# Nine blocks of dense weights converted during attention instead of ten, with other spacing of the conversions and of the early expert tiles

## The chip, the cores and the metric

The kernel runs on one core of one Trainium2 chip. The metric is the device time of one execution in microseconds (us). The kernel before takes 627.92 us, the median of three runs (627.23 to 629.49).

A core has five engines that work side by side, each through its own instructions in a fixed order: PE (TensorE, matmuls), DVE (VectorE), ACT (ScalarE), POOL (GpSimd) and SP (SyncE, which here only issues transfers). An instruction that waits holds up everything behind it on its engine. Transfers run on 16 DMA engines that all queues share. SBUF is the memory on the chip, PSUM the one that PE writes its results to.

## The reference

Three stages follow each other. Inputs are float32; the dense weights of the third stage arrive as 64-bit numbers.

```python
# 1 attention: 4 batches, 12 heads, 448 positions, 64 wide
scores = cap * np.tanh(scale * q @ k.T / cap)
attn = softmax(scores);  x = attn @ v            # -> 1792 tokens x 768
# 2 soft mixture of 8 experts with 4 slots each
logits = x @ phi                                 # 1792 x 32
d = softmax over tokens;  slot_in = d.T @ x      # 32 x 768
slot_out[e] = relu(slot_in[e] @ w1[e]) @ w2[e]   # w1: 768 x 1024, w2: 1024 x 768
x = softmax over slots(logits) @ slot_out
# 3 dense layers, width 2048
r = relu(x @ w_in);  out = (s * r * r + b) @ w_out
```

## The kernel before

**Stage 1, attention** (0 to 267 us of the profile). The 24 pairs of heads go through PE (scores, L498 and L515), ACT (tanh and exp, L521 and L535), PE again (times v, L556 and L564), and sums on DVE or POOL (L543, L549). Copies out of PSUM (`copy`, L421 on ACT, L423 on DVE) can go to either engine. Each pair loads its q, k and v rows (L432, L437/L438, L441/L446) through SP; there are two buffers for v, so a v load waits until PE has used up the pair two before it.

Two other things are slipped in beside attention. First, **conversions**: the weights of stage 3 are cut into 16 blocks of 128 columns, each block a tile of w_in and one of w_out. A tile arrives as 64-bit words (768 KB, L208). DVE picks the upper words apart in two instructions (L221, L224), ACT turns the lower words into numbers (L231), DVE or POOL adds the two (L234), and the float32 result (384 KB) is stored in a scratch tensor `scr` in DRAM (L342). `XS` is the number of blocks treated so, 2 x XS tiles; the others are converted in stage 3. Second, **early expert tiles**: ten tiles of w1 (1024 KB, L364) and four of w2 (768 KB, L370) are loaded into buffers that exist from the start. Six more w2 tiles have buffers in the space that the conversions use; they can be loaded only after the last conversion is stored (the step `cend`). Still more expert tiles go into space that attention gives up at its end.

**Stage 2, experts** (267 to 342 us). PE reads each expert tile once (L1008 for w1, L1029 for w2); when a tile is used up, its buffer takes the next one.

**Stage 3, dense** (from 342 us). Four passes over up to 512 tokens; in the first pass the 16 blocks must be ready one after the other. A block from `scr` is loaded as float32 (L1117). A block that is not in `scr` is loaded as words (L208) and goes through L221, L224, L231 and L234 here. Then the w_out tile is split into two parts (L1146/L1148, and L1151 on POOL), the w_in tile is multiplied with the slot outputs (L1160 to L1184, result `mst`), and each step x does a matmul (`h`, L1191), five elementwise operations (L1208 to L1236) and 24 large matmuls (`y`, L1254 and L1255).

**What sets the order.** `ListSchedule.run` (top of the file) is a planner that runs on the host while the kernel is built. Each operation has the engines it may run on with a duration in the planner's own units (a third number is a penalty for that engine), a priority, the buffers that it takes (`acq`) and gives back (`rel`), an earliest time (`after`) and a time that its result takes to be there (`lat`). The planner puts every operation behind the last one on its engine, earliest first; what it emits is fixed. It plans stage 1 and stage 3 separately.

The steps that the change touches stand at L293 to L297 (constants), L904 (`pn`), L906 to L912 (conversions: load `cl`, `ca`, `cf`, `cmul`, store `cst`) and L921 to L929 (early expert tiles `W`).

Of the kernel before, what the change touches and what calls it, by code (L numbers as in the profile page):

```python
# [28 lines left out]
ACT, DVE, POOL, PE, SP = "ACT", "DVE", "POOL", "PE", "SP"  # L29
# [73 lines left out]
def kernel(  # L103
# [17 lines left out]
    B, H, S, D = q.shape  # L121
# [45 lines left out]
    wide = w_in.dtype != F32  # L167
# [21 lines left out]
    MC = FF // FC  # L189
    NI = 2 * MC  # L190
    NE1 = KDM * FC
    XS = 10 if wide else 0
    scr_p = ctx.enter_context(tc.tile_pool(name="scr", bufs=1, space=bass.MemoryType.DRAM))
    scr = [scr_p.tile([128, NE1], F32, name=f"scr{i}") for i in range(2 * XS)]

# [97 lines left out]
    def run(safe):  # L293
        W1N, W2N = (4, (4,)) if safe else (10, (4, 6))
        NV, NEB, NES, NXU, NXQ, NQK = 2, 5, 2, 4, 3, 2
        PX, PA, DES, DESL, HACT = -0.32, 2.0, 1.0, 0.5, 0.5
        CV0, CVP, CVA, CVT, WA = 9.33, 2.0, 20.19, 9.5, 30.39  # L297
        LATE = 0.6

        PT, PDEN, PLG, PLW, PXT, PXM, PSO, PSL = -2.67, 1.0, 2.0, 3.4, 3.33, 2.05, 0.25, 4.75  # L300
# [22 lines left out]
        cx = ExitStack()  # L323
        cvs = range(0 if safe else 2 * XS)
        if cvs:
# [24 lines left out]
        def load_next():  # L350
            x = can_load()
            wq.remove(x)
            kind, e, c = x
            i = cnt[kind]
            cnt[kind] += 1
            n = sum(x for _, x in pools[kind])
            i %= n
            for pool, m in pools[kind]:
                if i < m:
                    break  # L360
                i -= m
            if kind == "w1":
                t = pool.tile([128, 2, FE], F32, tag="w1", name="w1c")
                nc.sync.dma_start(  # L364
                    out=t, in_=w1[e, 256 * c:256 * c + 256, :].rearrange("(p k) f -> p k f", p=128)
                )
                w1t[e, c] = t
            else:
                t = pool() if callable(pool) else pool.tile([128, 2, DM], F32, tag="w2", name="w2c")
                nc.sync.dma_start(  # L370
                    out=t, in_=w2[e, 256 * c:256 * c + 256, :].rearrange("(p k) f -> p k f", p=128)
                )
                w2t[e, c] = t
# [381 lines left out]
        def op(name, engs, f, need=(), prio=0.0, acq=(), rel=(), **kw):  # L755
            kw = {"lat": LATE if name[0] not in ("qk", "tanh", "exp", "qkl") else 0.2, **kw}
            sch.add(name, engs, lambda e: f(*name[1:], e), need, prio, acq, rel, **kw)
# [8 lines left out]
        for n in range(NP):  # L766
            f = 2 * n
            for w in "qk":
                i = ("ld", w, n)
# [3 lines left out]
            i = ("ld", "v", n)  # L773
# [58 lines left out]
        for g in range(NQ):  # L832
            bb, gq = divmod(g, NQUAD)
# [58 lines left out]
        for bb in range(B):  # L892
            g = NQUAD * (bb + 1) - 1
            pr = 4 * g + 4 + PSO
            prev = [("ssum", bb - 1)] if bb else []
            op(("soft", bb), [(PE, 0.38)], emit_soft, [("lgr", g)], pr, [("tp", ("soft", bb))], [("lw", g)])
            op(("smax", bb), [(DVE, 0.66)], emit_smax, [("soft", bb)] + prev, pr, [("nm", bb)])
            op(
                ("sexp", bb), [(ACT, 0.8)], emit_sexp, [("smax", bb)], pr, [("pt", bb), ("al", bb)],
                [("tp", ("soft", bb))],  # L900
            )
            op(("ssum", bb), [(DVE, 0.2)], emit_ssum, [("sexp", bb)] + [("pn", bb)] * (bb == B - 1), pr + 1, [], [("nm", bb), ("al", bb)])
            op(("softt", bb), [(PE, 0.33)], emit_softt, [("sexp", bb)], pr, [("tp", ("softt", bb))], [("pt", bb)])
            op(("pn", bb), [(DVE, 0.2)], emit_pn, [("softt", bb)], pr, [("pn", bb)], [("tp", ("softt", bb))])  # L904

        need = []  # L906
        for i in range(len(cvs)):
            pr = CV0 + CVP * i
            op(("cl", i), [(SP, 2.19)], cv_load, [], pr - 6, [("w", i)], lat=3.0, after=CVA + CVT * i)
            op(("ca", i), [(DVE, 1.55)], cv_a, [("cl", i)], pr, [("cm", i), ("ce", i)], [("w", i)], port=BOTH)  # L910
            op(("cf", i), [(ACT, 0.92)], cv_f, [("ca", i)], pr, [], [("w", i)])
            op(("cmul", i), [(DVE, 0.95), (POOL, 1.63)], cv_m, [("cf", i)], pr, [], [("ce", i)], port=BOTH)  # L912
            op(("cst", i), [(SP, 1.1)], cv_store, [("cmul", i)], pr, [], [("cm", i)], lat=LAT)
            need = [("cst", j) for j in range(i + 1)]
# [7 lines left out]
        first, n = W1N + W2N[0], W1N + sum(W2N)  # L922
        prev = []
        for i in range(n):
            sch.add(
                ("W", i), [(SP, 2.91 if i < W1N else 2.19)], lambda e: load_next(),
                prev + [("cend",)] * (i >= first), 1e3 + i, after=WA,
            )
            prev = [("W", i)]  # L929
        sch.run()  # L930
# [177 lines left out]
        def is_words(i):  # L1108
            return wide and (safe or i >= 2 * XS)

# [181 lines left out]
        for i in range(NI):  # L1292
            f, rows = divmod(i, 2)
            pr = float(f)
# [28 lines left out]
        if wide and not safe:  # L1323
            for i in range(NI):
                pr = MC + 2 + i
# [7 lines left out]
        prev = ["sot"]  # L1333
        for x, (t0, n, f) in enumerate(steps):
# [6 lines left out]
            for p in range(parts(x)):  # L1341
                i = (x, p)
# [9 lines left out]
            for t in range(nt):  # L1352
# [7 lines left out]
                prev = [("y", x, t)]  # L1360
# [5 lines left out]
        p2.close()  # L1366

    run(False)
    if dbg is None or "nosafe" not in dbg:
        big = nc.values_load(flag[0:1, 0:1], min_val=0, max_val=1)  # L1370
        with tc.If(big == 1):
            run(True)
# [30 lines left out]
```

## Time and profile before

| | us |
|---|---|
| median of 3 runs | 627.92 |
| the profiled execution | 627.3 |
| its span, first to last instruction | 625.5 |
| PE busy | 574.5 (92%) |
| ACT busy | 388.9 (62%) |
| DVE busy | 374.5 (60%) |
| POOL busy | 141.9 (23%) |
| mean granted TensorE clock | 0.964 |

The span is the time from the first to the last instruction; the execution's own time has 1.8 us around it. The shares of busy time are means over three stages with different limits. The DMA engines moved 139.25 MB, at 223 GB/s on the mean.

### The profile page before, as it was taken

The numbers are of one execution on the slowest core, as the hardware profiler recorded it, in microseconds if no ns is written. First come the engines' busy times: TensorE is split into PE (matmuls) and PEld (weight loads), VectorE is DVE, ScalarE is ACT, GpSimd is POOL, SyncE is SP. The second block draws the span as 40 slices with busy tenths as digits, with TensorE's granted clock in tenths as the row PEclk, the third lists the DMA queues.
The fourth block names the chain that finished last, engine by engine and source line by source line (L and its number), as shares of the span: only waits on it lengthen the run. The fifth ranks groups of instructions, "written<-read, shape, count | busy, mean of one in ns | idle before, by whom it ended". The sixth has DMA issues, their size and how long they took to land.

```text
span 625.5 us, 10133 instructions
## 1 busy us (share of the span) xinstructions
PE 574.5 (92%) x3982; PEld 356.5 (57%) x3982; DVE 374.5 (60%) x543; ACT 388.9 (62%) x550; POOL 141.9 (23%) x84
## 2 busy tenths in 40 slices
PE   6999897999999999799656899999999999999895
PEld 3333232334333433356323688888888888888784
DVE  2586566969999778635400599952676688511211
ACT  3977676778876987200000788886756566665783
POOL 0163264343854425100000824220000000000000
PEclk9999998999999999879977799999999999999998
DMA  8579999995576534999999985500988779000201
GB/s 152 137 236 296 323 287 326 306 269 154 163 240 175 166 97 146 409 418 415 416 418 410 361 298 178 183 2 28 352 276 257 246 254 353 2 2 1 101 1 56
DMA packets 103175, 139.25 MB, mean 223 GB/s; under 512 B 52432, under 2 KB 84944, under 8 KB 100048
## 3 DMA queue, kind: packets, MB, share of 16 engines
q1 hardware_dynamic: 102176, 138.43, 66.5%
q8 instruction: 33, 0.54, 0.3%
q10 hardware_dynamic: 944, 0.10, 0.1%
q14 instruction: 22, 0.18, 0.1%
HBM read 125.14 MB, written 13.37 MB: 221 GB/s over the span
## 4 chain that ended last, share of the span: by engine, by line
PE 61%; DMA 22%; DVE 10%; ACT 3%; issue 2%; SPq 1%; ACTq 0%; DVEq 0%
PE y L1254 25%; PE y L1255 12%; DMA w2c<-in_moe_w_dram 9%; PE sp L498 6%; PE av L556 5%; DMA w<-in_moe_w_in_dram 3%; PE tr L455 3%; DMA w<-scr 2%; DMA vn<-in_v_dram 2%; DMA w<-in_moe_w_out_dram 2%; DVE cm L224 2%; PE gp L1191 2%; DMA woe<-in_moe_w_dram 2%; DVE es L549 1%; PE av L564 1%
## 5 line engine op out<-in xcount | busy, mean ns | idle before, releaser
L1254 PE MATMUL y<-wo,gh 128*128 128x512 f32 x336 | 127.0, 400 | 0.0
L521 ACT ACTIVATE e<-sp,tsc 128x896 f32<-128x896 f32 x84 | 83.3, 1006 | 40.7 <-PE sp L498 28.0
L1236 DVE TENSOR_TENSOR gl<-r,gh 128x512 fp32r<-128x512 f32 (+1 forms) x65 | 42.6, 657 | 99.6 <-ACT r L1221 99.5
L1255 PE MATMUL y<-wo,gh 128*128 128x256 f32 x336 | 94.4, 281 | 0.0
L535 ACT ACTIVATE e<-e,capt 128x896 f32<-128x896 f32 x84 | 84.9, 1040 | 0.4
L498 PE MATMUL sp<-qs,ks 64*128 64x448 f32 x288 | 75.8, 606 | 0.0
L1254 PEld LDWEIGHTS y<-wo,gh 128*128 128x128 f32 x336 | 63.2, 188 | 13.8 <-issue 1.6
L1208 ACT ACTIVATE r<-gp 128x512 f32<-128x512 f32 (+1 forms) x65 | 34.9, 539 | 58.1 <-PE gp L1191 56.4
L556 PE MATMUL av<-e,vn 128*64 128x448 f32 x288 | 69.1, 562 | 1.8 <-DMA vn<-in_v_dram 1.8
L1254 PE MATMUL y<-wo,gl 128*128 128x512 f32 x168 | 66.6, 397 | 0.0
L1255 PEld LDWEIGHTS y<-wo,gh 128*128 128x128 f32 x336 | 63.2, 188 | 1.7
L275 DVE TENSOR_REDUCE rng<-w 128x1 f32<-128x768 f32 x64 | 56.9, 945 | 0.9 <-DMA w<-in_moe_w_in_dram 0.9
L543 POOL TENSOR_TENSOR es<-e 128x896 f32<-128x896 f32 x17 | 38.0, 2233 | 57.3 <-ACT e L535 28.1
L1221 ACT ACTIVATE r<-r,bt,st 128x512 f32<-128x512 f32 (+1 forms) x65 | 49.1, 757 | 1.8
L1221 ACT ACTIVATE gh<-r,bt,st 128x512 fp32r<-128x512 f32 (+1 forms) x65 | 49.1, 757 | 1.6
L1254 PE MATMUL y<-woe,gh 128*128 128x512 f32 x112 | 44.2, 416 | 3.2 <-ACT ob L1272 2.0
L1255 PE MATMUL y<-wo,gl 128*128 128x256 f32 x168 | 47.1, 281 | 0.0
L224 DVE SCALAR_TENSOR_TENSOR cm<-w,cm 128x768 int32<-128x768 int32 x32 | 45.8, 1430 | 1.1
L1146 ACT CAST woe<-w 128x768 fp32r<-128x768 f32 x2 | 1.7, 830 | 71.2 <-DMA w<-scr 71.2
L498 PEld LDWEIGHTS sp<-qs,ks 64*128 64x128 f32 x288 | 23.4, 193 | 35.6 <-issue 12.3
L543 POOL TENSOR_TENSOR es<-es,e 128x896 f32<-128x896 f32 x14 | 32.7, 2337 | 37.7 <-DVE es L543 20.8
L549 POOL TENSOR_TENSOR es<-es,e 64x448 f32<-64x448 f32 x23 | 30.8, 1340 | 42.3 <-DVE es L543 21.7
(153 smaller groups left out, 947.4 us busy)
## 6 DMA issues: line engine op xcount, KB each, us to landing
w<-in_moe_w_in_dram SPq DMA_DIRECT2D x32, 768.0 KB, 5.9
w<-in_moe_w_out_dram SPq DMA_DIRECT2D x32, 768.0 KB, 6.0
w1c<-in_moe_w_dram SPq DMA_DIRECT2D x24, 1024.0 KB, 13.1
w2c<-in_moe_w_dram SPq DMA_DIRECT2D x26, 768.0 KB, 16.5
scr<-cm SPq DMA_DIRECT2D x20, 384.0 KB, 4.4
w<-scr SPq DMA_DIRECT2D x20, 384.0 KB, 5.7
qn<-in_q_dram SPq DMA_DIRECT2D x24, 224.0 KB, 4.2
kn<-in_k_dram SPq DMA_DIRECT2D x24, 192.0 KB, 4.5
```

The source lines that it names most:

```text
L224: nc.vector.scalar_tensor_tensor(out=m, in0=hi, scalar=-0x40000000, in1=m, op0=ALU.bitwise_and, op1=ALU.bitwise_or)
L275: nc.vector.tensor_reduce(out=rng[:, j, i:i + 1], in_=hi, axis=AX.X, op=o, apply_absolute_value=True)
L498: nc.tensor.matmul(out=sp[:, h, 0:S], lhsT=ks[n][rows, 128 * j:128 * j + 128], rhs=qs[n][rows, :], start=True, stop=True,)
L521: nc.scalar.activation(out=e, in_=spt.pop((n, j))[:, :, 0:S], func=AF.Tanh, scale=tsc)
L535: nc.scalar.activation(out=e, in_=e, func=AF.Exp, scale=capt)
L543: eng.tensor_tensor(out=t, in0=et[n, 0] if j == 1 else t, in1=et[n, j], op=ALU.add)
L549: eng.tensor_tensor(out=t, in0=t, in1=et["l", n // 2][r:r + KL, n % 2], op=ALU.add)
L556: nc.tensor.matmul(out=avt[n][64 * h:64 * h + 64, 0:S], lhsT=vt[n][:, KC * h + j, :], rhs=et[n, j][:, h], start=(j == 0 and n % 2 == 0), s ...
L1221: nc.scalar.activation(out=out, in_=in_, func=AF.Identity, scale=st, bias=bt)
L1236: eng.tensor_tensor(out=gl, in0=t, in1=f32(gh), op=ALU.subtract)
L1254: nc.tensor.matmul(out=ya, lhsT=lhsT, rhs=w[:, 0:512], start=first, stop=last)
L1255: nc.tensor.matmul(out=yb, lhsT=lhsT, rhs=w[:, 512:768], start=first and i0 == 0, stop=last and i0 == per - 1)
```

## The change

XS goes from 10 to 9: 18 tiles instead of 20 are converted in stage 1, and block 9 (two tiles) joins the six blocks that are converted in stage 3. The conversions get priorities 1.85 apart instead of 2.0 and earliest times 8.5 apart instead of 9.5. A conversion's load is planned to take 6.0 units to land instead of 3.0. Each early expert tile gets an earliest time of its own, 5.0 units after that of the tile before it. The penalty for a copy on ACT goes from 0.5 to 0.2. The small copy `pn` is planned with 1.2 instead of 0.6 units, but for the last batch.

```diff
-    XS = 10 if wide else 0
+    XS = 9 if wide else 0
...
-        PX, PA, DES, DESL, HACT = -0.32, 2.0, 1.0, 0.5, 0.5
-        CV0, CVP, CVA, CVT, WA = 9.33, 2.0, 20.19, 9.5, 30.39
+        PX, PA, DES, DESL, HACT = -0.32, 2.0, 1.0, 0.5, 0.2
+        CV0, CVP, CVA, CVT, WA, WT = 9.33, 1.85, 20.19, 8.5, 30.39, 5.0
...
-            op(("pn", bb), [(DVE, 0.2)], emit_pn, [("softt", bb)], pr, [("pn", bb)], [("tp", ("softt", bb))])
+            op(("pn", bb), [(DVE, 0.2)], emit_pn, [("softt", bb)], pr, [("pn", bb)], [("tp", ("softt", bb))], lat=LATE if bb == B - 1 else 1.2)
...
-            op(("cl", i), [(SP, 2.19)], cv_load, [], pr - 6, [("w", i)], lat=3.0, after=CVA + CVT * i)
+            op(("cl", i), [(SP, 2.19)], cv_load, [], pr - 6, [("w", i)], lat=6.0, after=CVA + CVT * i)
...
-                prev + [("cend",)] * (i >= first), 1e3 + i, after=WA,
+                prev + [("cend",)] * (i >= first), 1e3 + i, after=WA + WT * min(i, first - 1),
```

Over stage 1 the planner now puts 23 copies on ACT and 73 on DVE (20 and 76 before), and 19 of the 47 large sums (L543) on DVE and 28 on POOL (16 and 31 before). The conversions' adds (L234) on POOL stay three. Until the fourteenth early expert tile SP issues nine conversion loads and seven stores in both kernels, and the fourteenth stands between the same two v loads.

The first place is SP's queue at the end of attention. `vn` are the v loads of a pair, `scr` a store of a converted tile, `w2c` and `w1c` expert tiles; the last `vn` pair is the last v load of all.

```order
-L342 DMA scr_116<-cm 128x768
-L441 DMA vn<-in_v_dram 128x2x192
-L446 DMA vn<-in_v_dram 64x64 x2
-L342 DMA scr_117<-cm 128x768
-L370 DMA w2c<-in_moe_w_dram 128x1536 x6
+L370 DMA w2c<-in_moe_w_dram 128x1536 x3
+L441 DMA vn<-in_v_dram 128x2x192
+L446 DMA vn<-in_v_dram 64x64 x2
+L370 DMA w2c<-in_moe_w_dram 128x1536 x3
+L441 DMA vn<-in_v_dram 128x2x192
+L446 DMA vn<-in_v_dram 64x64 x2
 L364 DMA w1c<-in_moe_w_dram 128x2048 x2
```

The last two stores are gone, and of the six w2 tiles that stood behind the last v load, three now stand before the last v load but one and three before the last one.

The second place is DVE at the first conversion, early in attention. `cm<-w` is the conversion's first work on a tile, `xu`, `dn` and `qs` are copies out of PSUM, `es` is a sum. First the kernel before:

```order
L423 COPY xu<-av 128x448
L221 TENSOR_SCALAR cm<-w_347 128x768
L224 SCALAR_TENSOR_TENSOR cm<-w_347,cm 128x768
L423 COPY dn<-dn 128x448
L543 TENSOR_TENSOR es<-e 128x896
L423 COPY dn<-lg 128x448
L423 COPY qs<-tr 128x448
```

and the changed one:

```order
L423 COPY xu<-av 128x448
L423 COPY dn<-dn 128x448
L543 TENSOR_TENSOR es<-e 128x896
L423 COPY dn<-lg 128x448
L423 COPY qs<-tr 128x448
L221 TENSOR_SCALAR cm<-w_345 128x768
L224 SCALAR_TENSOR_TENSOR cm<-w_345,cm 128x768
```

The conversion of the first tile now stands behind three copies and a sum that stood behind it; its load stands at the same place in SP's queue in both.

The third place is SP's queue at the start of stage 3, behind the fourteenth load from `scr`. `w<-scr` is a converted tile, `w<-in_moe_w_in_dram` and `w<-in_moe_w_out_dram` are tiles still to be converted. First the kernel before:

```order
L1117 DMA w_3357<-scr_111 128x768
L208 DMA w_3377<-in_moe_w_in_dram 128x6x256
L1117 DMA w_3393<-scr_112 128x768
L1117 DMA w_3405<-scr_113 128x768
L208 DMA w_3416<-in_moe_w_out_dram 128x1536
L1117 DMA w_3451<-scr_114 128x768
```

and the changed one:

```order
L1117 DMA w_3337<-scr_111 128x768
L208 DMA w_3357<-in_moe_w_in_dram 128x6x256
L208 DMA w_3373<-in_moe_w_out_dram 128x1536
L1117 DMA w_3398<-scr_112 128x768
L1117 DMA w_3415<-scr_113 128x768
L208 DMA w_3435<-in_moe_w_in_dram 128x6x256
```

The fourteen loads ahead are the same; behind them the tiles of words come closer together, and there are fourteen instead of twelve.

## Rows read from the trace of the kernel before

**Rows 1.** Stretches of the span (us): each engine's busy time, TensorE's clock, DMA.
```profile
25.00:250.00 225.00, 214.36 (x1252) 79.92 (x1252) 176.42 (x251) 171.86 (x199) 104.08 (x58) 0.99 0.76 227
250.00:267.00 17.00, 12.59 (x84) 5.39 (x81) 10.23 (x23) 3.94 (x7) 3.54 (x4) 0.87 1.00 408
267.00:342.00 75.00, 56.97 (x928) 33.39 (x920) 22.62 (x47) 0.63 (x1) 0.00 (x0) 0.84 1.02 416
357.00:420.00 63.00, 62.85 (x455) 51.17 (x454) 54.32 (x62) 53.37 (x94) 21.31 (x11) 1.00 0.53 180
420.00:626.00 206.00, 195.27 (x1102) 169.09 (x1100) 94.82 (x129) 132.98 (x208) 0.00 (x0) 0.99 0.43 146
```
Columns: the stretch and its length, PE, weight loads of PE, DVE, ACT, POOL busy (instructions), granted clock, DMA share, GB/s.

**Rows 2.** The chain of waits, in order of time: start, length, what.
```profile
26.48 5.50 DMA w<-in_moe_w_in_dram
...
61.01 8.97 DMA vn<-in_v_dram
...
85.33 8.55 DMA w<-in_moe_w_out_dram
...
266.99 12.66 DMA woe<-in_moe_w_dram
...
333.25 11.48 DMA w<-scr
```

**Rows 3.** Waits of PE between 300 and 342 us: total, times, longest.
```profile
PE h1p L1008 <- DMA w1c<-in_moe_w_dram: 8.6, 6, 3.6
PE so L1029 <- DMA w2c<-in_moe_w_dram: 5.0, 5, 1.1
```

**Rows 4.** SP's issues in order of time: a late v load, the six w2 tiles.
```profile
231.29 0.37 SPq L441 DMA_DIRECT2D vn<-in_v_dram  x1
...
248.00 4.68 SPq L370 DMA_DIRECT2D w2c<-in_moe_w_dram  x6
```

**Rows 5.** The w2 tiles issued between 247 and 252 us: issue to landing.
```profile
DMA to landing us min/median/max: 4.7/6.5/9.4
```

**Rows 6.** Stretches of attention behind late conversion loads, columns as in rows 1.
```profile
30.00:35.00 5.00, 3.73 (x26) 1.30 (x24) 2.96 (x4) 3.56 (x5) 0.00 (x0) 1.00 0.78 259
90.00:100.00 10.00, 6.18 (x44) 1.90 (x40) 7.15 (x11) 5.71 (x8) 3.59 (x2) 0.93 1.06 348
...
140.00:145.00 5.00, 4.28 (x25) 1.90 (x21) 4.02 (x6) 5.00 (x7) 0.00 (x0) 1.00 0.44 121
```

**Rows 7.** Instructions by line: count, busy us, mean ns, idle before.
```profile
L543 DVE TENSOR_TENSOR es<-es,e 128x896 f32<-128x896 f32 x9 | 9.8, 1087 | 4.2 <-POOL es L549 3.3 <-ACT e L535 0.9
...
L423 DVE COPY xu<-av 128x448 f32<-128x448 f32 x17 | 10.5, 620 | 4.6 <-PE av L564 3.0 <-PE av L556 1.4
```

**Rows 8.** DVE in the first dense pass: start, length, instruction, idle before it.
```profile
380.04 2.04 DVE L221 TENSOR_SCALAR cm<-w 128x768 int32<-128x768 int32 x1
382.11 2.50 DVE L224 SCALAR_TENSOR_TENSOR cm<-w,cm 128x768 int32<-128x768 int32 x1
384.53 0.55 DVE L221 TENSOR_SCALAR cm<-w 128x768 int32<-128x768 int32 x1
385.11 0.96 DVE L224 SCALAR_TENSOR_TENSOR cm<-w,cm 128x768 int32<-128x768 int32 x1
...
387.24 1.83 DVE L234 CUSTOM_DVE_ANT_0 cm<-cm,ce 128x1536 uint16<-128x1536 uint16 x2
...
417.01 0.29 DVE L1184 TENSOR_TENSOR mst<-gp,mst 64x128 fp32r<-64x128 f32 x1 [2.38 <-ACT mst L1181]
```

**Rows 9.** PE in order of time: the matmul that needs the last block.
```profile
424.14 0.40 PE L1191 MATMUL gp<-cs,mst 128*128 128x512 f32 x1
```

**Rows 10.** The stretch of the conversions in the first dense pass, columns as in rows 1.
```profile
358.80:417.30 58.50, 58.50 (x432) 47.63 (x431) 51.88 (x59) 50.53 (x91) 19.51 (x10) 1.00 0.54 183
```

**Rows 11.** PE's first use of a late v tile, in order of time.
```profile
241.34 0.97 PE L556 MATMUL av<-e,vn 128*64 128x448 f32 x4
```

**Rows 12.** The v loads between 205 and 256 us: issue to landing.
```profile
DMA to landing us min/median/max: 2.0/2.5/3.2
```

## The prediction

> **What bounds the kernel now.** I read the stretches of the span first. In attention (25 to 250 us) PE is busy 214.36 of 225 us at nearly full clock; no engine has more to do, and 10.6 us is all that this stretch could lose if PE never waited. In the expert stretch (267 to 342 us) PE is busy 56.97 of 75 us and the DMA engines are full at 416 GB/s: transfers bound it. In the first dense pass (357 to 420 us) PE is busy 62.85 of 63 us, and it stays nearly so afterwards [rows 1].
>
> Then the chain of waits, to see how the stretches hang together. Attention ends at 267 us. From there the chain runs through transfers alone: an expert tile that is issued at 266.99 us lands 12.66 us later, further expert tiles follow, and the last link, 11.48 us to a converted tile, starts the dense stage [rows 2]. So the dense stage starts when the DMA engines have worked off what stood in line. The waits of PE say the same: between 300 and 342 us it stood 8.6 us for w1 tiles and 5.0 us for w2 tiles, 13.6 us in all [rows 3].
>
> Last, what filled that line before 267 us. SP issues six w2 tiles at 248.00 us, one behind the other, all behind the last v load [rows 4]. The DMA engines move 408 GB/s from 250 us on [rows 1] and are still behind when attention ends.
>
> **The change part by part.**
>
> *The six w2 tiles.* They now stand in SP's queue before the last two v loads. The last v load but one went out at 231.29 us [rows 4], so three of the tiles go out before that and three between the two v loads. Six tiles of 786 432 bytes are 4.72 MB, 11.3 us at the 416 GB/s of the expert stretch [rows 1]; that is the most that can be gained, and nothing is the least, if the stores ahead of them come late. What stands behind them, the tiles in the space that attention gives up, cannot be issued much sooner, so the DMA engines may run dry before 267 us. I therefore price the gain by the tile that waited: it took 12.66 us [rows 2], and a w2 tile that finds an empty line takes 4.7 us [rows 5]. The line is shorter by 12.66 - 4.7 = 8.0 us. PE can use all of it, since it stood 13.6 us for tiles [rows 3]. Term: **-8.0 us**, ends -11.3 and 0.
>
> What these six tiles could hold up is the v load behind each three of them. Three tiles are 2.36 MB, 5.7 us at 416 GB/s. The v load of 231.29 us takes up to 3.2 us [rows 12] and is first used at 241.34 us [rows 4, 11]: 6.8 us are left over. Cost 0; without that cover, 5.7 us each.
>
> *The conversions' planned landing, 6.0 instead of 3.0.* With 2.19 for the issue a load now has 8.2 units before DVE is to take it up, as against 5.2. In the trace a first one takes 5.50 us, a later one 8.55 us [rows 2]. While DVE stands before such a tile, the copies that PE wants stand behind it. Behind three late loads PE lost 1.3, 3.8 and 0.7 us [rows 6]. A lead longer by 3 can give back at most 1.3 + 3.0 + 0.7 = 5.0 us. The 8.55 us load would be late under the new lead too, so I take half, -2.5 us.
>
> *Sums and copies.* By the order DVE gets three large sums more, 3 x 1.087 = 3.3 us, and three copies less, 3 x 0.620 = 1.9 us [rows 7]: +1.4 us, on an engine that is often what PE waits for. The three copies cost ACT no more than DVE, and ACT is idle for 53 of 225 us [rows 1]: 0.
>
> *Two conversions less, at denser times.* They go at the end of attention, where their place is taken by nothing; that gives DVE room that I count at 0, because the tail from 250 to 267 us is a string of small steps that has no conversion in it.
>
> *The early expert tiles' spacing.* By the order the fourteenth stands between the same v loads, behind as many conversion loads as before. Cost 0, and the v load of 8.97 us on the chain [rows 2] stays.
>
> For attention together: -2.5 + 1.4 = **-1.1 us**. The plan of a whole stage has moved, which no row shows; the ends are all that PE lost, -10.6 us, and one more v load on the chain like that of 8.97 us, +9.0 us. I take the value near 0, because PE's busy time there doesn't change.
>
> *Block 9 converted in the dense stage.* One block on DVE is five rows: 2.04 + 2.50 + 0.55 + 0.96 + 1.83 = 7.9 us [rows 8]. DVE had 58.50 - 51.88 = 6.6 us idle in that stretch [rows 10]. The last block was ready at 417.3 us [rows 8], and the matmul that needs it came at 424.14 us [rows 9]: 6.8 us of slack. 7.9 us is covered by idle time and slack together. Term: **0**. Were both tiles as slow as the first here (2 x (2.04 + 2.50 + 0.92) = 10.9 us) and no idle time usable, 10.9 - 6.8 = +4.1 us would come out on PE. The block's transfers add 0.8 MB to a stretch whose DMA share is 0.53 [rows 1], and the fourteen loads that start the stage are the same: 0. Below nothing I see no end, since no engine has less to do there.
>
> One rule speaks against this part. The first tile's two instructions took 2.04 and 2.50 us, the second's 0.55 and 0.96 us, of the same shapes [rows 8]. The Trainium skill ("SBUF — State Buffer", Who interferes with whom) says that VectorE and GpSimd share a port pair as an exclusive lock: a VectorE instruction that wants the pair waits for the whole GpSimd instruction. The trace agrees, with 0.55 us alone and 2.04 us otherwise. By that rule each added tile can meet a POOL split, which is the end at +4.1 us and a total of 622.3 us.
>
> **The sum** is made against the profiled execution, 627.3 us (span 625.5 us and 1.8 us around it), 0.1% below the median of 627.92 us: 627.3 - 8.0 - 1.1 + 0 = **618.2 us**, 1.5% below.
>
> **The rivals.**
>
> *The gain is given back in attention.* The conversions come denser (8.5 instead of 9.5 apart), into a stretch with a DMA share over 1 [rows 6]. If one more v load comes late like the 8.97 us one, 627.3 - 8.0 + 9.0 = 628.3 us. For it speaks that the spacing of the early tiles hardly moved; against it, that up to the fourteenth SP issues as many loads as before. Chance 0.18.
>
> *The six tiles don't come early.* If SP stands at the store ahead of them until the end of attention, only -1.1 us is left: 626.2 us. Against it: there are two conversions less, and they end sooner. Chance 0.06.
>
> *Block 9 comes too late.* With the +4.1 us above: 627.3 - 8.0 - 1.1 + 4.1 = 622.3 us. For it speaks that block 9 is due a step sooner than block 10 was. Chance 0.10.
>
> *Slower: v loads behind blocked rows of SP.* A conversion load waits for its buffer in SP's queue, and the v loads wait behind it; the denser they come, the oftener. With two more v waits of 8.97 us on the chain the time is 627.3 - 8.0 + 17.9 = 637.2 us. It decides from 8 us of new v waits on. Against it: v loads late in attention land in 2.5 us [rows 12]. Chance 0.11.
>
> **How the numbers follow.** The forecast has 0.55. It and block 9 too late are faster by over 0.5%, which is about what a measurement of this kernel can tell from no change (3.1 us); given back and not early are mostly within it, each with a little on the faster side. That makes 0.67 faster, 0.21 the same, 0.12 slower. The range reaches down to the most that tiles and attention bear out together short of both ends (-11.3 and half of -10.6 us with a little room: 609 us), and up over the given-back case to 629 us; the slower rival stays outside. The forecast's own range is 612 to 624 us.
>
> **What would show it.** In the profile after: the six w2 tiles go out before about 235 us, and the expert tile at attention's end lands within 6 us; PE's waits for expert tiles shrink from 13.6 to about 6 us; the expert stretch is 8 us shorter. Attention ends between 263 and 268 us. In the first dense pass PE stays busy without a wait for block 9. I am wrong if attention ends later than 272 us, or if PE waits over 3 us for a conversion in the dense stage.

## The result, and the profile after

The changed kernel takes 619.34 us (median of 4 runs, 618.73 to 619.54); the kernel before took 627.58 us on the same chip (627.12 to 629.49). The ratio is 0.9861, 95% interval 0.9839 to 0.9884. The forecast was 618.2 us, so the total is 1.1 us off. Its terms were off by up to 2.4 us and made up for each other, so a total this near is luck.

The profiled executions have spans of 625.5 us before and 617.4 us after, 8.1 us apart. Two starts divide the span: the first expert matmul (L1008) ends attention, the first dense matmul (L1160) ends the expert stretch.

| piece of the span | before, us | after, us | change | forecast |
|---|---|---|---|---|
| up to the first expert matmul | 269.7 | 266.4 | -3.3 | -1.1 |
| from there to the first dense matmul | 73.1 | 67.5 | -5.6 | -8.0 |
| from there to the end | 282.7 | 283.5 | +0.8 | 0 |

The same stretches of the kernel after as in [rows 1]: length, PE, weight loads of PE, DVE, ACT, POOL busy with instructions, granted clock, DMA share, GB/s.

```profile
25.00:250.00 225.00, 218.21 (x1277) 80.83 (x1275) 172.97 (x250) 172.64 (x200) 96.78 (x56) 0.99 0.82 246
250.00:267.00 17.00, 10.94 (x82) 4.52 (x78) 8.39 (x21) 2.50 (x6) 0.98 (x2) 0.83 0.71 276
267.00:342.00 75.00, 60.53 (x958) 36.07 (x948) 25.12 (x49) 5.61 (x15) 5.53 (x3) 0.84 0.99 397
357.00:420.00 63.00, 63.00 (x442) 52.12 (x441) 49.68 (x61) 52.55 (x91) 17.34 (x9) 1.00 0.43 142
```

In attention PE's idle time went from 10.6 us to 225 - 218.21 = 6.8 us. At the end of attention the DMA share fell from 1.00 to 0.71: the line of transfers that stood there before is gone, and from 250 to 255 us there is little in its place:

```profile
250.00:255.00 5.00, 4.33 (x26) 1.58 (x19) 0.37 (x2) 1.60 (x3) 0.00 (x0) 1.00 0.32 85
```

Cut finer, attention shows where PE stood. First the kernel before:

```profile
25.00:45.00 20.00, 18.73 (x104) 6.37 (x100) 13.71 (x21) 17.18 (x19) 8.82 (x4) 1.00 0.75 220
45.00:135.00 90.00, 83.32 (x477) 31.04 (x476) 64.79 (x95) 63.63 (x73) 39.71 (x23) 0.98 1.02 306
135.00:250.00 115.00, 112.31 (x676) 42.52 (x676) 97.92 (x136) 91.06 (x108) 55.54 (x32) 1.00 0.56 167
```

and the kernel after:

```profile
25.00:45.00 20.00, 20.00 (x113) 7.05 (x110) 13.85 (x19) 17.35 (x20) 8.00 (x4) 1.00 0.94 268
45.00:135.00 90.00, 87.60 (x508) 32.49 (x508) 69.61 (x102) 70.48 (x84) 36.35 (x21) 0.98 1.05 312
135.00:250.00 115.00, 110.61 (x658) 41.29 (x660) 89.51 (x131) 84.80 (x98) 52.44 (x31) 1.00 0.62 192
```

PE's idle time by stretch was 1.3, 6.7 and 2.7 us; it is 0, 2.4 and 4.4 us. Most of the gain lies in the stretch where the DMA share is over 1 in both kernels.

What DVE waited for among transfers there (25 to 265 us: total, times, longest), before:

```profile
DVE cm L221 <- DMA w<-in_moe_w_in_dram: 8.4, 4, 2.9
DVE cm L221 <- DMA vn<-in_v_dram: 3.3, 1, 3.3
DVE cm L221 <- DMA w<-in_moe_w_out_dram: 1.7, 1, 1.7
```

and after:

```profile
DVE cm L221 <- DMA scr<-cm: 3.3, 1, 3.3
DVE cm L221 <- DMA w<-in_moe_w_out_dram: 0.8, 1, 0.8
```

DVE's first conversion instruction stood 13.4 us behind transfers before and 4.1 us after; of conversion loads (the rows with `w`) 0.8 us are left, from 10.1 us.

SP's issues around the end of attention, after, which answer to [rows 4] (start, length of the issues together, what):

```profile
215.99 3.06 SPq L370 DMA_DIRECT2D w2c<-in_moe_w_dram  x3
...
227.85 1.53 SPq L370 DMA_DIRECT2D w2c<-in_moe_w_dram  x3
...
236.94 8.60 SPq L364 DMA_DIRECT2D w1c<-in_moe_w_dram  x2
...
252.46 1.28 SPq L370 DMA_DIRECT2D w2c<-in_moe_w_dram  x3
...
253.79 11.00 SPq L370 DMA_DIRECT2D woe<-in_moe_w_dram  x4
```

What SP itself waited for between 230 and 270 us, after:

```profile
SPq L370 <- PE sl L723: 9.1, 2, 8.7
SPq L364 <- PE sp L498: 7.6, 1, 7.6
SPq L370 <- PE av L556: 6.7, 1, 6.7
...
SPq L364 <- PE h1p L1008: 3.5, 1, 3.5
```

The six w2 tiles go out 20 to 32 us sooner, as forecast. Of the tiles behind them the two w1 tiles go out some 16 and 8 us sooner, at 236.9 and 245.2 us, the rest by 2 to 5 us. SP is held 7.6 us before the second w1 tile, 6.7 us before the next w2 tiles and 8.7 us before the last `woe` tiles, until PE has finished with the buffers of attention. In part of that time the DMA engines run dry. After attention's end the next w1 tile stands 3.5 us until PE has used up an expert tile (L1008).

PE's waits between 300 and 342 us, after, for [rows 3]:

```profile
PE h1p L1008 <- DMA w1c<-in_moe_w_dram: 4.6, 3, 3.6
PE so L1029 <- DMA w2c<-in_moe_w_dram: 4.2, 4, 1.3
```

And the long links of the chain of waits, after, for [rows 2]:

```profile
50.09 8.93 DMA scr<-cm
...
81.43 8.09 DMA vn<-in_v_dram
...
290.11 16.98 DMA w2c<-in_moe_w_dram
...
307.15 17.59 DMA w2c<-in_moe_w_dram
...
324.75 11.47 DMA w<-scr
```

The 12.66 us transfer at 266.99 us is gone. From 266 to 290 us the chain now runs through PE, and transfers bound the kernel only from 290 us on. The first 8 us of that, after (the kernel before moved 416 GB/s there):

```profile
267.00:275.00 8.00, 8.00 (x116) 4.15 (x110) 3.57 (x9) 0.63 (x1) 0.00 (x0) 0.73 0.85 316
```

How much had still to be moved between attention's end and the first dense matmul? The length of the expert stretch times the GB/s in it says so, for both kernels and three of the experiments below:

| kernel | expert stretch, us | GB/s in it | moved, MB |
|---|---|---|---|
| before | 73.1 | 415 | 30.3 |
| e5: after, tiles held until 247 us | 73.5 | 415 | 30.5 |
| after | 67.5 | 403 | 27.2 |
| e1: after, tiles at 236 us | 67.3 | 401 | 27.0 |
| e2: before with nine blocks | 67.9 | 400 | 27.2 |

### The profile page after: what moved, and what is told of

Its sections match the earlier page's. It is cut to its first block, busy times and chain, and to the rows that moved or that the text cites. A ratio compares the mean times of both kernels' runs of the same rounds, so it can differ in the third digit from the quotient of the medians.

```text
span 617.4 us, 10121 instructions
## 1 busy us (share of the span) xinstructions
PE 573.8 (93%) x3982; PEld 355.4 (58%) x3982; DVE 369.5 (60%) x543; ACT 388.8 (63%) x553; POOL 132.4 (21%) x81
## 4 chain that ended last, share of the span: by engine, by line
PE 74%; DMA 12%; DVE 9%; ACT 2%; POOL 1%; issue 1%; SPq 0%; POOLq 0%; DVEq 0%; ACTq 0%
PE y L1254 25%; PE y L1255 12%; PE sp L498 8%; PE av L556 7%; DMA w2c<-in_moe_w_dram 6%; PE tr L455 3%; DMA w<-scr 2%; PE h1p L1008 2%; PE gp L1191 2%; PE dn L586 2%; PE rowt L599 2%; PE lg L614 2%; PE sp L515 1%; DVE cm L224 1%; DMA scr<-cm 1%; DMA vn<-in_v_dram 1%
## 5 line engine op out<-in xcount | busy, mean ns | idle before, releaser
L1236 DVE TENSOR_TENSOR gl<-r,gh 128x512 fp32r<-128x512 f32 (+1 forms) x65 | 43.9, 677 | 95.6 <-ACT r L1221 95.5
L224 DVE SCALAR_TENSOR_TENSOR cm<-w,cm 128x768 int32<-128x768 int32 x32 | 43.8, 1368 | 1.1
L543 POOL TENSOR_TENSOR es<-es,e 128x896 f32<-128x896 f32 x15 | 32.2, 2145 | 48.5 <-PE tr L455 13.2
L543 POOL TENSOR_TENSOR es<-e 128x896 f32<-128x896 f32 x13 | 27.6, 2124 | 57.3 <-ACT e L535 37.8
L1215 ACT ACTIVATE r<-r 128x512 f32<-128x512 f32 (+1 forms) x65 | 37.1, 573 | 1.7
```

Of the source, the lines that this page charges most:

```text
L224: nc.vector.scalar_tensor_tensor(out=m, in0=hi, scalar=-0x40000000, in1=m, op0=ALU.bitwise_and, op1=ALU.bitwise_or)
L543: eng.tensor_tensor(out=t, in0=et[n, 0] if j == 1 else t, in1=et[n, j], op=ALU.add)
L1215: nc.scalar.activation(out=t, in_=t, func=AF.Square)
L1236: eng.tensor_tensor(out=gl, in0=t, in1=f32(gh), op=ALU.subtract)
```

## The experiments

Ratios are to the kernel before, run on the same chip in the same set. "After" is the changed kernel, 619.34 us; it was not run again in the later sets, where the kernel before has medians of 626.1 to 627.2 us, so a difference from after of 1 us says little.

**e1: the six w2 tiles behind the last v load.** From after:

```diff
-                prev + [("cend",)] * (i >= first), 1e3 + i, after=WA + WT * min(i, first - 1),
+                prev + [("cend",), ("ld", "v", NP - 1)] * (i >= first), 1e3 + i, after=WA + WT * min(i, first - 1),
```

> The changed kernel, with the six w2 tiles behind the last v load again; every other engine's order stays word for word. Theory (early tiles shorten the expert stretch): the expert tile at attention's end takes about 12 us to land instead of a few, the expert stretch (first expert matmul to first dense matmul) goes from 67.5 us back to about 73 us, attention keeps its end at 266 us: 619.3 + 5.6 = 625 us. Rival (the gain came from less conversion work in attention, the tiles were hidden anyway): 619 us, expert stretch 67 to 68 us.

619.09 us (617.62 to 620.07), ratio 0.9869 (0.9836 to 0.9903): a miss, with the rival's total and stretch; e5 tests the rival's reason. SP's row:

```profile
236.00 3.30 SPq L370 DMA_DIRECT2D w2c<-in_moe_w_dram  x6
```

Behind the last v load the tiles go out at 236 us, not at 248 us, and that is early enough: the expert stretch is 332.9 - 265.6 = 67.3 us. The place before the v loads, which the order showed, is worth nothing. In the kernel before it wasn't the v loads that held the tiles, but the last conversion store, which stood in SP's queue just ahead of them and went out at 247.6 us:

```profile
247.63 0.33 SPq L342 DMA_DIRECT2D scr<-cm  x1
```

That after issues the tiles 8 to 20 us sooner still isn't what counts either: in e1 the DMA engines still move 396 GB/s at the end of attention, and what is left for the expert stretch is the same (27.0 MB).

```profile
250.00:267.00 17.00, 10.95 (x81) 4.58 (x82) 9.01 (x21) 2.55 (x7) 0.98 (x2) 0.77 0.97 396
```

**e2: the kernel before with nine blocks, nothing else.**

```diff
-    XS = 10 if wide else 0
+    XS = 9 if wide else 0
```

> The kernel before with XS = 9 and nothing else of the change. SP then has two w2 tiles before the last v load and four behind it. Theory (what counts is when the six tiles go out, and a longer lead of the conversions for attention): expert stretch 68 to 70 us, attention's end unchanged within 1 us of 269.7 us (first expert matmul), about 623.5 us. Rival (the two conversions taken out of attention are the gain): attention 3 us shorter, the whole gain, 619 us.

621.42 us (620.37 to 622.02), ratio 0.9897 (0.9864 to 0.9930). Its w2 tiles:

```profile
231.37 2.59 SPq L370 DMA_DIRECT2D w2c<-in_moe_w_dram  x2
...
240.04 2.17 SPq L370 DMA_DIRECT2D w2c<-in_moe_w_dram  x4
```

Attention ends at 268.8 us (-0.9), the expert stretch is 67.9 us (-5.2), the rest 283.2 us. This one number brings nearly the whole gain of the expert stretch. DVE still waits for conversion loads, 12.7 us as against 10.1 before. The total is 2 us under the theory's 623.5 us.

**e3: after without the longer lead.**

```diff
-            op(("cl", i), [(SP, 2.19)], cv_load, [], pr - 6, [("w", i)], lat=6.0, after=CVA + CVT * i)
+            op(("cl", i), [(SP, 2.19)], cv_load, [], pr - 6, [("w", i)], lat=3.0, after=CVA + CVT * i)
```

> The changed kernel with the planned landing of a conversion load at 3.0 again. Theory (the longer lead took DVE's waits for conversion loads from 13.4 to 0.8 us and gave attention 3.3 us): those waits come back to about 10 us, first expert matmul at 269 to 270 us instead of 266.4, about 622.5 us. Rival (the lead does nothing, attention got shorter by the two conversions less): 619 us, whatever the waits are.

629.46 us (626.46 to 631.96), ratio 1.0025 (1.0004 to 1.0046). The direction is right and the size is far off: attention ends at 277.7 us, 11.3 us later than after (the profiled run took 631.7 us, 2.2 more than the median). The finer stretches, for those of before and after above:

```profile
25.00:45.00 20.00, 17.59 (x99) 5.93 (x95) 13.84 (x20) 15.15 (x17) 8.24 (x4) 1.00 0.81 252
45.00:135.00 90.00, 83.89 (x483) 31.26 (x481) 63.87 (x94) 66.92 (x78) 41.47 (x24) 0.98 1.01 302
135.00:250.00 115.00, 108.87 (x639) 39.97 (x637) 88.43 (x120) 84.30 (x99) 57.78 (x34) 0.97 0.62 187
```

PE is idle 2.4, 6.1 and 6.1 us, 14.6 in all, as against 6.8 in after. Beside e2 this also prices the rest together: the denser conversions, the tiles' spacing, the copies and `pn`, on top of nine blocks and without the lead, cost 629.46 - 621.42 = 8.0 us; the lead then gives back 629.46 - 619.34 = 10.1 us. What each of the four does alone isn't shown here.

**e4: the kernel before, with block 9 also converted in the dense stage** (the work in attention is as before; the result stored there for block 9 isn't used).

```diff
-            return wide and (safe or i >= 2 * XS)
+            return wide and (safe or i >= 2 * XS - 2)
```

> The kernel before, with block 9 converted in the dense stage as well as in attention (its two scratch tiles are stored and not read). Attention and the expert stretch are as before. Theory (idle time and slack cover the block): from the first dense matmul to the end 282.7 us plus 0 to 1 us, 627.5 to 628.5 us. Rival (the block comes late on DVE): plus 4 us, 631.5 us.

626.10 us (624.12 to 631.00), ratio 1.0013 (0.9977 to 1.0049). From the first dense matmul to the end it takes 283.1 us, 0.4 us more than before. The +4.1 us of the forecast's third rival are not there. The total is under the theory's 627.5 us, as the kernel before was under 627.3 us in this set (626.99 us).

**e5: after, with the six w2 tiles held until about 247 us** by a small store whose data DVE writes then.

```diff
+        hold = scr_p.tile([P, R * NS], F32, name="hold")
+        def hold_store(_):
+            nc.sync.dma_start(out=hold, in_=lall[:, B - 1].rearrange("p r c -> p (r c)"))
+        op(("hold",), [(SP, 0.4)], hold_store, [("lgr", B * NQUAD - 2)], 1e3)
...
-                prev + [("cend",)] * (i >= first), 1e3 + i, after=WA + WT * min(i, first - 1),
+                prev + [("cend",), ("hold",)] * (i >= first), 1e3 + i, after=WA + WT * min(i, first - 1),
```

> The kernel after, plus one small store (112 x 128 numbers of the sums of the last batch element, 57 KB to scratch memory) that the six w2 tiles wait for. Its data are written by VectorE at about 245 us, so SP stands at it as it stood at the last conversion store in the kernel before, and the tiles go out at about 246 us, not at 216 to 228. The previous run showed that 236 us is early enough. Theory (what the tiles cost in the kernel before was standing behind a late store until 248 us): attention ends as in after (266 us), the expert stretch goes back from 67.5 us towards the 73.1 us of before, total 624 to 625 us. Rival (the gain of the expert stretch has to do with other things, such as fewer conversion stores and loads at the end of attention, not with when the tiles are issued): 619 to 620 us. Second rival: SP at the store holds back something that attention itself needs, and attention ends later than 268 us.

626.19 us (623.31 to 628.06), ratio 0.9992 (0.9960 to 1.0024). SP's rows:

```profile
246.91 0.35 SPq L925 DMA_DIRECT2D hold<-lall  x1
247.31 3.13 SPq L370 DMA_DIRECT2D w2c<-in_moe_w_dram  x6
```

and the end of attention:

```profile
250.00:267.00 17.00, 10.95 (x78) 4.58 (x76) 8.13 (x20) 2.50 (x6) 0.98 (x2) 0.83 1.02 422
```

Attention ends at 266.7 us as in after, the expert stretch is back at 340.2 - 266.7 = 73.5 us, and the DMA share at its end is full again. With everything else of the change in place, holding SP's queue until 247 us at these tiles costs 6 us of the stretch. What stands behind them is held too (the first of the two w1 tiles goes out at 250.49 us, not at 236.94), as it was behind the store in the kernel before. That settles the first term's mechanism.

**e6: the kernel before with the longer lead alone** (the edit of e3 the other way round).

> The kernel before with one edit, the planned landing of conversion loads 6.0 and not 3.0. Theory (the lead is what moved attention, since without it the kernel after lost 11 us there): VectorE's waits for conversion loads fall from 13.4 us to under 5 us, attention ends 3 to 5 us sooner, at about 265 us; the six w2 tiles still stand behind the last conversion store, so the expert stretch stays at 73 us; total 623 to 625 us. Rival (the lead matters only in the denser plan of nine blocks, where it repairs what the new spacing breaks): attention ends at 269 to 271 us and the total is 627 us.

623.15 us (619.32 to 627.59, 10 runs), ratio 0.9956 (0.9914 to 0.9999): the theory's total, though the interval all but reaches no change. The profiled run was the fastest of the ten, so its rows say more than the median bears out: DVE waits 0.8 us for conversion transfers, attention ends at 264.2 us, and the expert stretch is still 70.9 us. With e2 (-5.6 us) this -3.0 us comes to about the whole change of -8.2 us. That the two add up is argued and not shown: nine blocks and the lead without the rest weren't run, and by e3 and e9 the rest isn't without effect.

**e7: after with a lead of 8.0** (`lat=8.0` in the same line).

> The kernel after with the planned landing of conversion loads at 8.0, not 6.0. VectorE's waits for conversion loads in attention are 0.8 us already in after, so theory: nothing more to gain, attention ends at 265 to 268 us, the total is 618 to 621 us. Rival (every longer lead takes load off the crowded stretch from 45 to 135 us, also for v tiles and stores): attention ends at 262 us and the total is 615 us. Third: the loads come so early that their buffers and the v loads behind them are late, 623 us or more.

616.63 us (615.49 to 617.53), ratio 0.9841 (0.9781 to 0.9902). Attention ends at 262.7 us, near the first rival's 262 us, and the total lies between the theory and that rival. Conversion loads aren't waited for at all any more; PE's idle time from 25 to 250 us falls from 6.8 to 4.8 us.

**e8: after with the early expert tiles 10 apart, not 5.**

```diff
-        CV0, CVP, CVA, CVT, WA, WT = 9.33, 1.85, 20.19, 8.5, 30.39, 5.0
+        CV0, CVP, CVA, CVT, WA, WT = 9.33, 1.85, 20.19, 8.5, 30.39, 10.0
```

> The kernel after with the first fourteen expert tiles planned 10 units apart, not 5, so that by the order they are spread as far as 165 of the planned units and no longer stand together between 30 and 110. Theory: the chain of after still holds 8.93 us for a store and 8.09 us for a v load in the stretch where the DMA engines are full; with 14 tiles (13.6 MB, 33 us at 416 GB/s) spread, these shorten, and attention ends 2 to 5 us sooner, total 614 to 617 us. Rival (the DMA engines are full there for conversions and the heads' own loads, or PE waits for something else in it): attention ends at 265 to 268 us, total 618 to 621 us. Second rival: the tiles come now beside the loads of late attention and take from them, 622 us or more.

615.01 us (614.01 to 617.11), ratio 0.9826 (0.9764 to 0.9889), as the theory said. The crowded stretch:

```profile
45.00:135.00 90.00, 88.00 (x519) 32.68 (x518) 67.51 (x102) 71.30 (x83) 44.06 (x24) 1.00 0.94 286
135.00:250.00 115.00, 112.71 (x666) 42.86 (x665) 88.05 (x130) 84.65 (x100) 49.97 (x30) 1.00 0.72 222
```

The DMA share there falls from 1.05 to 0.94, PE's idle time in the two stretches from 2.4 and 4.4 to 2.0 and 2.3 us, and attention ends at 262.3 us. The v load of 8.09 us is no longer on the chain. The intervals of e7 and e8 overlap that of after; it is their traces that bear out the gain.

**e9: after with the copies' preference of before** (`HACT` 0.5, not 0.2).

> The kernel after with the copies' preference as before (ScalarE priced 0.5 over VectorE, not 0.2). Theory: VectorE gets some copies back at 0.62 us each, ScalarE has the room anyway; the prediction priced the pieces of work that change engine at +1.4 us for attention, so without them attention ends at 264 to 267 us and the total is 618 to 619.5 us. Rival (copies on ScalarE are what lets VectorE keep up with the denser conversions): attention ends at 269 us or later, total 622 us or more.

622.64 us (618.40 to 625.48, 12 runs), ratio 0.9925 (0.9896 to 0.9954): the rival's number, attention ends at 271.0 us. But not for the rival's reason: DVE has 73 copies and ACT 23 in both kernels up to 270 us. What differs is which ones and where, and three large sums (16 on DVE, 19 in after). The chain shows what was late:

```profile
60.11 10.10 DMA vn<-in_v_dram
...
119.08 7.06 DMA scr<-cm
```

Behind these two PE does 6.86 us of work between 65 and 75 us and 7.43 us between 125 and 135 us. Five of the twelve runs took 618.4 to 620.0 us, the other seven 622.4 to 625.5 us. Why they part there wasn't traced. Both late transfers stand in the stretch from 45 to 135 us, whose DMA share is 1.00; in after it is 1.05, so the share alone doesn't tell the two apart.

**e10: after with eight blocks** (`XS = 8`).

> The kernel after with eight blocks converted in attention, not nine, so that one more block of five VectorE instructions (7.9 us by the rows of before) comes into the first dense pass. There VectorE is busy 49.7 of 63 us in after. Theory: attention has two conversions less and the last ones end sooner (attention ends 1 us sooner, 265 us), the expert stretch stays at 67 us, and the dense pass has 13 us of idle VectorE for 8 us of work but not at the right times: the dense stretch grows by 1 to 4 us, total 619 to 622 us. Rival (the dense pass takes a tenth block as it took the ninth, at 0.8 us or less): 617 to 618.5 us. Second rival (VectorE becomes the bound there): 624 us or more.

623.28 us (619.46 to 627.30, 12 runs), ratio 0.9962 (0.9936 to 0.9988), between the theory and the second rival. In the profiled run, the fastest one, attention ends at 263.9 us and the expert stretch is 66.8 us, but from the first dense matmul to the end it takes 287.0 us, 3.5 more than after. PE waits there:

```profile
PE y L1254 <- DVE gl L1236: 2.4, 3, 1.2
```

Of the 1.3 us of slack that were left for the last block in after (worked out below) 0.2 us are left (418.68 - 418.48). Nine is the better number here.

**e11: e7 and e8 together.**

> The kernel after with both edits that were faster than it: expert tiles planned 10 apart and the landing of conversion loads at 8.0. Theory: both take their gain from the same place, PE's waits in attention; after e7 and e8 PE stands there only for small things, so together they give no more than the better one: attention ends at 261 to 263 us, total 613.5 to 616 us. Rival (they add up, 2.7 and 4.3 us): 612 us. Second rival (a plan of a whole stage that moves again, by chance for the worse): 618 us or more.

614.04 us (612.34 to 614.67), ratio 0.9809 (0.9780 to 0.9839), as the theory said: 1 us below e8 alone, which their intervals don't tell apart. PE from 135 us on:

```profile
135.00:250.00 115.00, 114.48 (x677) 43.10 (x676) 89.44 (x136) 87.55 (x103) 47.89 (x27) 1.00 0.75 225
```

It is idle for 0.5 us there. This is the fastest version of the case: 5.3 us below after by the medians, 0.9809 / 0.9861 = 0.9947 by the ratios, whose intervals just touch.

**e12: e11 with the early tiles from 100 units on, 6 apart.**

```diff
-        CV0, CVP, CVA, CVT, WA, WT = 9.33, 1.85, 20.19, 8.5, 30.39, 10.0
+        CV0, CVP, CVA, CVT, WA, WT = 9.33, 1.85, 20.19, 8.5, 100.0, 6.0
```

> The kernel of e11 (landing of conversion loads at 8.0) with the first fourteen expert tiles planned from 100 units on, 6 apart, not from 30.39 on, 10 apart: none of them stands any more in the stretch from 45 to about 110 us, where the DMA share is 0.97 in e11 and 1.05 in after. Theory (what PE still loses in attention hangs on transfers that land late where the DMA engines are full; tiles in that stretch are the movable part of it): the DMA share of 45 to 135 us falls to about 0.85, and PE, which lost 2.8 us there in e11 and 2.4 us in after, loses under 1.5 us; from 135 us on the share rises from 0.75 to about 0.85, still under 1; attention ends at 260 to 261.5 us, total 612 to 614 us. Rival (what is left there has to do with the order of the work on VectorE and GpSimd, not with transfers): attention ends at 261.5 to 263 us, 614 to 615.5 us. Second rival (the tiles now meet the last conversions and the v loads of late attention): 617 us or more.

620.87 us (618.44 to 621.65), ratio 0.9888 (0.9857 to 0.9919). The theory is right up to 135 us and the second rival behind it:

```profile
45.00:135.00 90.00, 89.30 (x524) 33.12 (x520) 78.23 (x106) 72.23 (x86) 34.76 (x20) 1.00 0.77 225
...
135.00:155.00 20.00, 18.40 (x115) 6.95 (x112) 13.45 (x24) 15.91 (x21) 11.22 (x7) 1.00 1.10 329
155.00:175.00 20.00, 18.11 (x113) 6.46 (x113) 16.58 (x22) 14.33 (x18) 10.76 (x6) 1.00 1.08 343
```

and on the chain:

```profile
141.45 7.62 DMA vn<-in_v_dram
...
162.74 8.52 DMA vn<-in_v_dram
```

PE loses 0.7 us where the DMA share is 0.77, and 1.6 and 1.9 us in the two stretches where it is now over 1, behind v loads that landed sooner there in e11. From 135 to 250 us it loses 7.8 us in all, 0.5 in e11. 4.3 us of that is one wait for ACT from 191.5 to 195.9 us: ACT had itself stood 3.95 us for PE at a copy (L421), with the next tanh and exp behind it. That a late transfer lies behind this wait isn't shown. The crowd moved, and a loss of PE of 3.5 us behind v loads moved with it.

## Why the prediction was right, and where its terms were off

*What bounds the kernel.* Right: the dense stage starts when the expert tiles are through, and the line ahead of them was made by six tiles issued late. e5 shows it by putting the line back (+6 us).

*The six w2 tiles, -8.0 us; measured -5.6 (e2: -5.2, e5: -6.0).* The mechanism was right, the size was not, and the place in the order wasn't the reason (e1). By the table, 30.3 - 27.2 = 3.1 MB less were left to move when attention ended. That is 7.6 us at 415 GB/s, near the 8.0 us by which the line was to be shorter, though the 8.0 came from one tile's wait and not from bytes; the rest of the six tiles' 4.7 MB wasn't gained, as SP stood at the tiles behind them for want of buffers. The step that failed is "PE can use all of it, since it stood 13.6 us for tiles". With the line gone, the transfers wait for PE in turn: from 267 to 275 us PE is busy for all 8.00 us, the next w1 tile stands 3.5 us for a buffer, and the DMA engines move 316 GB/s and not 416. Over the expert stretch that leaves 403 GB/s in place of 415, which is 0.8 MB or 2.0 us; so the 5.6 us that came split into 7.6 - 2.0. The same paragraph saw that the engines "may run dry before 267 us" and gave it no price. They do (276 GB/s from 250 to 267 us), but e1, where they move 396 GB/s there, has the same stretch: what counts is how many bytes are left, and how fast they can go from there on. PE's waits for w1 and w2 tiles between 300 and 342 us fell from 13.6 to 8.8 us, not to 6.

*The lead, -2.5 us, and the sums and copies, +1.4 us; together -1.1, measured -3.3.* The lead's half of 5.0 us was too small. I counted the losses behind three late loads and took the late 8.55 us load as late again; after the change DVE waits 0.8 us for conversion loads in all. Alone the lead is worth 3.0 us at the median (e6), in the plan of after 10.1 us (e3). The +1.4 us, as a sum of durations on DVE, is not what came. The large sums (L543) did grow, from 15.2 to 18.5 us between 25 and 250 us. But the small sums (L549) fell from 21.0 to 14.2 us and the conversions (L221, L224, L234) from 61.6 to 58.0 us, so DVE's busy time fell from 176.42 to 172.97 us; why L549 got shorter wasn't traced. And e9, with three large sums fewer on DVE and as many copies, is 3.3 us slower and has two late transfers on its chain. A plan's price isn't the sum of the instructions that change engine.

*Given back in attention (0.18).* It didn't happen, but something like it is in the change: without the lead the rest of it costs 8.0 us (e3 against e2), near the +9.0 us that was worked out. That the sizes meet is luck, since e3's chain holds no late v load but late conversion loads, of 10.29 us at 99.44 us and 8.98 us at 110.44 us. The change contains both the damage and its repair.

*Block 9, 0 us; measured +0.8 (e4: +0.4).* Right in kind: idle time and slack cover it. The last block's result and the matmul that needs it, for [rows 8, 9], after:

```profile
414.25 0.29 DVE L1184 TENSOR_TENSOR mst<-gp,mst 64x128 fp32r<-64x128 f32 x1 [2.23 <-ACT mst L1181]
```

```profile
415.85 0.40 PE L1191 MATMUL gp<-cs,mst 128*128 128x512 f32 x1
```

Of 6.8 us of slack 415.85 - 414.54 = 1.3 us are left, and one block more costs time (e10). The end at +4.1 us, from the rule on the port pair in the Trainium skill ("SBUF — State Buffer", Who interferes with whom), didn't come about. The rule itself agrees with the trace after. The first instruction of a conversion on DVE takes 0.55 us alone [rows 8]; beside POOL:

```profile
406.02 2.22 DVE L221 TENSOR_SCALAR cm<-w 128x768 int32<-128x768 int32 x1
```

and POOL's instruction there:

```profile
405.80 2.02 POOL L1151 TENSOR_TENSOR wo<-cm,wo 128x768 fp32r<-128x768 f32 x1 [5.35 <-ACT wo L1146]
```

But such meetings became fewer. Of a conversion's first two instructions (L221, L224) in the first dense pass eight of 24 took over 1.7 us before, and five of 28 after; together they took 30.0 us for twelve tiles and 28.8 us for fourteen. That was luck of the order: nothing in the prediction said that the added block would cost DVE no time.

*Slower through blocked v loads (0.11).* Not in after. e9 is 3.3 us slower than after with one late v load on its chain, e12 6.8 us slower than e11 with two, but these loads are long from their issue on (10.10, 7.62 and 8.52 us); that a conversion load's wait in SP's queue held them isn't shown.

Of the marks set down for the profile, five came as written: the tiles out before 235 us, the tiles at attention's end landing within 6 us (`woe` tiles issued at 263.7 and 264.5 us, in 4.2 and 5.3 us), the end of attention between 263 and 268 us, no wait for block 9, no wait over 3 us for a conversion in the dense stage. Two did not: PE's waits, and the expert stretch, which is shorter by 5.6 and not 8 us.

## What to carry to other kernels

When a line of transfers is what ends a stage, price an earlier issue in bytes: how many fewer are left when the stage starts, and how fast they can go from there on, since once the line is gone the transfers wait for buffers in turn. Ask of a blocked queue which instruction holds it (here a store behind late work, not the loads that stand next to it): moving that one was worth the 5 to 6 us here, and the place before the v loads nothing. Where a stage slips in optional transfers, plan their landing for the crowded stretch and spread them so that no stretch is over full: that was worth another 3 to 5 us here (e7, e8, e11), and moving the crowd to another stretch lost 6.8 us again (e12).

## What was unexpected of the hardware

The same v load (192 KB) lands in 2.5 to 3.4 us (median 2.8) between 135 and 250 us of after, where the DMA share is 0.62, and in 5.5 to 9.2 us (median 7.4) between 45 and 135 us, where it is 1.05. In e12, from 135 to 195 us with a share of 1.10 and 1.08 in the first two thirds, it is 7.6 to 9.8 us (median 8.6); in e11 it was 2.7 to 7.3 us (median 5.1) there.

How much runs of one kernel differ isn't the same for every plan. In one set on one chip e11 lies within 2.3 us in 6 runs, e9 and e10 spread over 7.1 and 7.8 us in 12, and the kernel before over 6.7 us in 23; why isn't shown. One profile of a kernel of the second sort can be 3.8 us from its median (e6, e10), and a term of 2 us can't be read from it.
